# Packing the low half of the softmax weights mid-block, with shifted copies of v, in a fused attention and two-MLP kernel

## The chip, the core and the metric

The kernel runs on one core of one Trainium2 chip. The metric is device time in microseconds (us), the median of several executions; smaller is better. TensorE is written PE (its weight loads PEld), VectorE DVE, ScalarE ACT, GpSimd POOL, SyncE SP. Nearly all DMAs are issued by SP, in order.

## The reference, cut to what matters

For 4 batches of 8 heads with 576 tokens and 64 columns a head:

```
scores = q @ k.T / 8;  cum = cumsum(max(s, 0))
scores = where(causal, -1e9, scores + min(cum[j] - cum[i], 0))
p = exp(scores - max);  p = p / (sum(p) + 1e-9)
x = p @ v                                        # (4, 576, 512)
u = x + real(fft(fft(x, tokens), features))
y = u + relu(layernorm(u) @ w1) @ w2             # first MLP, 512 -> 2048 -> 512
out = y + relu((layernorm(y) * g) @ w3) @ w4     # second MLP
```

The weights w1 to w4 arrive in 64-bit floating point, everything else in float32.

## The kernel before, in words

Accuracy is kept by splitting each float32 operand of a product into a high and a low half in f16 and adding three products: high with high, high with low, low with high.

A pair is two heads of one batch; there are 16. The 576 rows of a pair's attention are five kinds of tile: A0, A1, M, B1 and B0, which see 129, 257, 320, 448 and 576 keys (`EXT`, line 27). A unit is one kind of tile of one head. `emit_qk32` or `emit_qk` makes the scores, `emit_exp` (line 832) lets ACT write the high half of p in f16 and p itself in float32, `emit_lo` (line 856) lets POOL (in batch 1, for B0, DVE) write the low half behind it. The high half fills `NKB` blocks of 128 columns (2, 3, 3, 4, 5), zeros included, and so does the low half. One DMA transpose (line 864, or 872 for both heads of A0, A1 and M) turns all blocks, and `emit_pv` (line 875) multiplies each: three matmuls for each of the `NKB` blocks, 64 columns wide. B0's and B1's p tiles get their zero columns from POOL in each unit (line 843), the others once. The tile `P.v` holds v as 5 blocks of 128 rows, high and low, written by `split_v` (line 1061): ACT the high half, then DVE the low half.

`attn_steps32` runs batches 0 and 1, `attn_steps` batches 2 and 3. `fft_steps` follows each batch, and the first MLP runs on chunks of 256 or fewer rows: `emit_ln` (line 383) normalises a chunk, splits it into `u16` and has it transposed to `unT`; `emit_g1` and `emit_g2` are its two products. While the first MLP of batch b runs, attention and FFT of batch b+1 are interleaved with it. Batch 0's attention has no MLP beside it; in its place DVE, ACT and POOL convert w1 and w2 (class `Weights`, lines 176 to 260). The second MLP (`Weights7`, `emit_g1x`, `emit_g2x`) follows when attention is over; its weights are opened by `open_wb` (line 1377), which closes the attention pools and opens a pool in their place.

The order of instructions on each engine is fixed when the kernel is compiled: a planner simulates the program and sorts by simulated time and priority, and each engine then takes its list in order.

Of the kernel before, what the change touches and what calls it, by code (L numbers as in the profile page):

```python
# [26 lines left out]
EXT = [129, 257, 320, 448, 576]  # L27
NKB = [2, 3, 3, 4, 5]
MASKED = -(2.0 ** 120)
# [4 lines left out]
def fused_kernel(ctx: ExitStack, tc, q, k, v, s, wa1, wa2, g_ln, wb1, wb2, tok_c, feat_c, ident_c, rev_c, bias_c, out):  # L34
    nc = tc.nc

    const = ctx.enter_context(tc.tile_pool(name="const", bufs=1))
    wpool = ctx.enter_context(tc.tile_pool(name="wpool", bufs=1))
# [13 lines left out]
    FW = [130, 258, 320, 448, 576]  # L52
    HW = [512, 768, 768, 1024, 1280]

# [3 lines left out]
    def htile(name, t, h, which):  # L58
        return ring.tile([128, HW[t]], F16, tag=f"h{which}{t}{h}", name=name)

    probs = {}

    def htile2(name, t, which):
        if which:
            return ring.tile([128, 2 * HW[t]], F16, tag=f"h{which}{t}", name=name)
        if t not in probs:
            w = probs[t] = ring.tile([128, 2 * HW[t]], F16, name=f"p16{t}")
            nc.gpsimd.memset(w.rearrange("p (r w) -> p r w", r=4)[:, :, EXT[t]:], 0.0)
        return probs[t]
# [4 lines left out]
    def fwide(name):  # L74
        turn["f"] += 1
        if turn["f"] % 2:
            return ftile(name, B0, turn["f"] // 2 % 2)
        return htile(name, B0, turn["f"] // 2 % 2, 1).bitcast(F32)

# [30 lines left out]
    class Weights:  # L110
# [271 lines left out]

    def emit_ln(ch):
# [18 lines left out]
        nc.vector.tensor_scalar(out=mp, in0=mv[:, :, 0], scalar1=-1.0, scalar2=None, op0=ALU.mult)  # L402
        ch.last = nc.vector.tensor_tensor(out=mb, in0=mp, in1=p, op=ALU.mult)
        yield
        ch.unT = mpool.tile([128, 8, 256], F16, tag="unT", name="unT")
        for j in range(n):
            u16 = mpool.tile([128, 1024], F16, tag="u16", name="u16")
            nc.scalar.activation(
                out=u16[:, 0:512], in_=xs[j], func=AF.Identity, scale=p[:, j:j + 1], bias=mb[:, j:j + 1]
            )  # L410
# [421 lines left out]
    def emit_exp(u, mn):  # L832
# [5 lines left out]
        u.rs = sums[0][:, 2 * (u.k % 2):2 * (u.k % 2) + 2]  # L838
        w = NKB[t] * 128
        if t in (B0, B1):  # L840
# [15 lines left out]
    def emit_lo(u):  # L856
        t = u.t
        n, w = EXT[t], NKB[t] * 128
        eng = nc.gpsimd if t in KN["LO_POOL"][u.p // NPAIR] else nc.vector
# [16 lines left out]
    def emit_pv(u):  # L876
# [7 lines left out]
        ps = pvt[0]  # L884
        nb = NKB[t]
        pT = u.pT[:, 0:2 * nb * 128].rearrange("p (b n) -> p b n", n=128)
        c = slice(64 * h, 64 * h + 64)
        n = 0
        for kb in range(nb):

            for lp, lv in ((0, 0), (0, 1), (1, 0)):
                nc.tensor.matmul(  # L892
                    out=ps[:, c], lhsT=pT[:, lp * nb + kb, :], rhs=P.v[:, kb, lv, c],
                    start=(n == 0), stop=(n == 3 * nb - 1),
                )
                n += 1
        if h == 1:
# [123 lines left out]
    def prep_pair32(p):  # L1021
# [14 lines left out]
        for t in range(4):  # L1036
# [12 lines left out]
        nc.scalar.activation(  # L1049
            out=P.v[:, :, 0, :].bitcast(BF16), in_=rv, func=AF.Square, accum_out=mx[:, 2:3]  # L1050
        )
# [6 lines left out]
    def v_tile():  # L1058
        return att.tile([128, 5, 2, 128], F16, tag="v16", name="v16", bufs=2)

    def split_v(P, rv):
        nc.scalar.activation(out=P.v[:, :, 0, :], in_=rv, func=AF.Copy, scale=P.sc[:, 2:3])
        nc.vector.scalar_tensor_tensor(
            out=P.v[:, :, 1, :], in0=rv, scalar=P.sc[:, 2:3], in1=P.v[:, :, 0, :], op0=ALU.mult, op1=ALU.subtract
        )

    def emit_qk32(u):
# [309 lines left out]
    def open_wb(ch):  # L1377
        att_stack.close()
        wpool2 = ctx.enter_context(tc.tile_pool(name="wpool2", bufs=1))
        gt = const.tile([128, KB], F32, name="gt")  # L1380
        nc.sync.dma_start(out=gt, in_=g_ln.rearrange("(k p) -> p k", p=128))
# [20 lines left out]
    if True:  # L1402
# [59 lines left out]
        first = chunks1(0)  # L1462
        for n, _ in enumerate(urgent(emit_ln(first[0]), KN["LNOFF"][0])):
            weights_after((list(KN["QL"]) + [0] * 9)[n], first[0].last)
        attns = {1: gated(urgent((attn_steps32 if N32 > 1 else attn_steps)(1), KN["A1OFF"]), wa.mark)}
        for b in range(B):
            chunks = first
            if b + 1 < B:
                first = chunks1(b + 1)

                def gens(b=b):
# [97 lines left out]
```

## Time and profile before

| | us |
|---|---|
| median of 3 runs | 1078.03 (1076.03 to 1079.23) |
| the profiled execution, own time | 1075.65 |
| its span, first to last instruction | 1073.9 |
| PE busy | 970.5 (90%), granted clock 0.96 of full |
| DVE, ACT, POOL busy | 670.2, 594.3, 457.5 |

Busy time is that of the engine's own instructions. A wait is idle time of an engine put down to the instruction or DMA that ended it. The clock column is the granted clock of TensorE, 1.00 for 2.4 GHz and 0.50 for 1.2 GHz; a value between is a mean over a stretch that had both.

### The profile page before, as it was taken

How to read it: one execution, taken by the hardware profiler on the slowest of the kernel's cores; microseconds unless marked ns; L12 is line 12 of the kernel's file. 1: busy time of each engine (PE TensorE's matmuls, PEld its weight loads, DVE VectorE, ACT ScalarE, POOL GpSimd, SP SyncE). 2: the span in 40 equal slices, each digit the busy share in tenths (PEclk: the TensorE clock that was granted, in tenths of full speed). 3: DMA queues.
4: the chain of work that ended last, by engine and by line, in shares of the span. 5: the costliest groups of instructions: out<-in, count | busy, mean ns of one | idle time of the engine just before them, and what ended most of it. 6: DMA issues, size and time to landing. Idle time of an engine off the chain costs nothing.

```text
span 1073.9 us, 22892 instructions
## 1 busy us (share of the span) xinstructions
PE 970.5 (90%) x8665; PEld 741.5 (69%) x8665; DVE 670.2 (62%) x1655; ACT 594.3 (55%) x1271; POOL 457.5 (43%) x766
## 2 busy tenths in 40 slices
PE   4677668999989899789999989899999999999998
PEld 3454345777656676457666656578888888888887
DVE  5989878667775564956659978744543553542342
ACT  5788668775686753877534465444444444443341
POOL 3535334555365451535610052454544544543452
PEclk9779877999999999999999999999999999999999
DMA  6999965888589970699934852021112111111000
GB/s 194 268 184 283 219 166 113 175 156 134 118 161 183 205 150 2 138 200 161 207 89 137 294 168 61 21 59 21 41 43 38 40 46 36 40 40 21 21 21 21
DMA packets 289063, 125.47 MB, mean 117 GB/s; under 512 B 272696, under 2 KB 272952, under 8 KB 286904
## 3 DMA queue, kind: packets, MB, share of 16 engines
q1 hardware_dynamic: 288312, 121.90, 51.3%
q0 software_dynamic: 640, 2.10, 0.7%
q8 instruction: 68, 1.11, 0.4%
q14 instruction: 43, 0.35, 0.1%
HBM read 61.50 MB, written 9.51 MB: 66 GB/s over the span
## 4 chain that ended last, share of the span: by engine, by line
PE 38%; DVE 7%; DMA 2%; ACT 2%; issue 1%; SPq 0%; DVEq 0%; ACTq 0%
PE acc L538 15%; PE g1x L510 9%; PE g L510 9%; PE g L468 2%; PE g L444 2%; DMA unT<-u 1%; DVE wblow L189 1%; DMA wbbig<-in_moe_w_ch_dram 1%; DVE wblow L192 1%; DVE h L451 1%; DVE wbbig L369 1%; DVE st L394 0%; ACT wbrows L239 0%; DVE wbrows L192 0%; DMA xset<-x2d 0%
## 5 line engine op out<-in xcount | busy, mean ns | idle before, releaser
L444 PE MATMUL g<-unT,warows 128*128 128x256 f16 (+1 forms) x1920 | 220.9, 266 | 4.3 <-DMA unT<-u 4.3
L444 PEld LDWEIGHTS <-warows 128*128 128x128 f16 x1920 | 175.2, 100 | 44.3 <-DMA unT<-u 3.9
L468 PE MATMUL g<-wastage,h 128*128 128x512 f16 x756 | 184.6, 383 | 10.1 <-ACT h L450 6.7
L510 PEld LDWEIGHTS <-wbrows 128*128 128x128 f16 x1728 | 169.1, 98 | 20.2
L860 POOL TENSOR_TENSOR p<-sc,p 128x448 f16<-128x448 f32 (+4 forms) x152 | 140.5, 934 | 95.5 <-ACT sc L850 79.5
L524 DVE TENSOR_TENSOR wastage<-wastage 128x896 f16<-128x896 f32 x72 | 78.5, 1090 | 161.3 <-ACT wastage L523 161.3
L538 PEld LDWEIGHTS <-wastage 128*128 128x128 f16 x1512 | 147.9, 98 | 17.1
L468 PEld LDWEIGHTS <-h 128*128 128x128 f16 x864 | 83.0, 99 | 101.3 <-DVE h L451 11.8
L523 ACT CAST wastage<-wastage 128x896 f16<-128x896 f32 x72 | 67.5, 938 | 117.1 <-POOL wastage L521 117.1
L849 ACT ACTIVATE p<-sc,mn 128x129 f16<-128x129 f32 (+4 forms) x160 | 89.1, 576 | 46.7 <-DVE mn L816 20.7
L520 POOL TENSOR_TENSOR wastage<-wastage 128x128 f32<-128x128 f32 x72 | 50.5, 702 | 133.9 <-ACT wastage L517 133.9
L510 PE MATMUL g1x<-unT,wbrows 128*128 128x256 f16 x864 | 101.5, 273 | 0.0
L510 PE MATMUL g<-unT,wbrows 128*128 128x256 f16 x864 | 100.9, 273 | 0.0
L892 PEld LDWEIGHTS <-pT 128*128 128x128 f16 x1632 | 64.8, 101 | 47.8 <-DMA pT<-p 30.3
L892 PE MATMUL pv<-v,pT 128*128 128x64 f16 x1632 | 70.6, 198 | 28.0 <-DMA pT<-p 22.7
L850 ACT ACTIVATE sc<-sc,mn 128x129 f32<-128x129 f32 (+4 forms) x160 | 91.6, 573 | 1.1
L538 PE MATMUL acc<-wbbig,wastage 128*128 128x256 f16 x756 | 89.9, 273 | 0.0
L538 PE MATMUL acc<-wblow,wastage 128*128 128x256 f16 x756 | 87.9, 273 | 0.0
L797 POOL TENSOR_SCALAR_AFFINE_SELECT sc<-cumb 128x129 f32<-128x129 f32 (+4 forms) x120 | 63.8, 544 | 46.4 <-ACT cumb L713 30.1
L1084 PE MATMUL s<-first 128*128 128x288 f32 (+4 forms) x192 | 74.7, 489 | 5.0 <-DVE mn L1089 3.5
L451 DVE SCALAR_TENSOR_TENSOR h<-g,h 128x512 f16<-128x512 f32 (+1 forms) x80 | 50.5, 631 | 33.6 <-ACT h L450 33.1
L450 ACT ACTIVATE h<-g 128x512 f16<-128x512 f32 (+1 forms) x80 | 43.4, 543 | 32.3 <-PE g L444 31.9
(238 smaller groups left out, 1529.3 us busy)
## 6 DMA issues: line engine op xcount, KB each, us to landing
wbbig<-in_moe_w_ch_dram SPq DMA_DIRECT2D x8, 1024.0 KB
wbbig<-in_moe_w_ch_dram SPq DMA_DIRECT2D x16, 512.0 KB
cumb<-cumd SPq DMA_DIRECT2D x24, 288.0 KB
wastage<-in_moe_w_ch_dram SPq DMA_DIRECT2D x6, 1024.0 KB
xset<-in_moe_w_ch_dram SPq DMA_DIRECT2D x9, 512.0 KB
x2d<-o SPq DMA_DIRECT2D x18, 256.0 KB
first<-in_q_dram SPq DMA_DIRECT2D x64, 64.0 KB
first<-in_k_dram SPq DMA_DIRECT2D x32, 128.0 KB
```

The source lines that it names most:

```text
L444: nc.tensor.matmul(out=ps[:, c * i:c * i + c], lhsT=ch.w.w1(lw, kk, m + i), rhs=ch.unT[:, 4 * lx + kk, 0:c], start=(n == 0), stop=(n == 23),)
L468: nc.tensor.matmul(out=ch.ps[j], lhsT=h[:, lh, c:c + 128], rhs=ch.w.w2(lw, m + i), start=(m + i + n == 0), stop=(m + i == MB - 1 and n == 2),)
L510: nc.tensor.matmul(out=ps, lhsT=ch.w.w1(lw, kk, m + 8 * half), rhs=ch.unT[:, 4 * lx + kk, :], start=(n == 0), stop=(n == 11),)
L523: nc.scalar.copy(out=h[:, 0], in_=r[:, 0:7])
L524: nc.vector.tensor_tensor(out=h[:, 1], in0=r[:, 0:7], in1=h[:, 0], op=ALU.subtract)
L538: nc.tensor.matmul(out=acc[key], lhsT=h[:, lh, ia], rhs=b[:, ib, lw], start=(m == 0 and i == 0 and not second), stop=(m == 7 and i == 2 an ...
L797: nc.gpsimd.affine_select(out=u.f[:, 0:n], in_=P.cumb[u.h][:, 0:n], pattern=[[-1, n]], compare_op=ALU.is_ge, fill=MASKED, base=base, chann ...
L849: nc.scalar.activation(out=u.w[:, 0:n], in_=u.f[:, 0:n], func=AF.Exp, bias=mn, scale=-1.0)
L850: nc.scalar.activation(out=u.f[:, 0:n], in_=u.f[:, 0:n], func=AF.Exp, bias=mn, scale=-1.0, accum_out=u.rs[:, h:h + 1])
L860: eng.tensor_tensor(out=u.w[:, w:w + n], in0=u.f[:, 0:n], in1=u.w[:, 0:n], op=ALU.subtract)
L892: nc.tensor.matmul(out=ps[:, c], lhsT=pT[:, lp * nb + kb, :], rhs=P.v[:, kb, lv, c], start=(n == 0), stop=(n == 3 * nb - 1),)
L1084: nc.tensor.matmul(out=ps, lhsT=P.qT[:, QCOLS[t]], rhs=P.kT[h][:, a:z], start=not pe, stop=not masked,)
```

## The change

For A0, A1, M and B0 the high half now ends in the middle of a block (`HALF` = 192, 320, 320, 576 columns) and the low half begins there, so that both together take 3, 5, 5 and 9 blocks in place of 4, 6, 6 and 10. B1 stays at 4 and 4. A low half that begins 64 columns into a block meets v shifted by 64 rows, so `P.v` grows from 5 to 9 blocks: DVE copies v's high rows shifted by 64 into blocks 7 and 8, and rows for the one mixed block (`MIX`) into blocks 4 to 6, four copies a pair. A mixed block takes two matmuls (with v's high and its low), a full pair of blocks three as before. B0's p tile now has no zero columns to fill. In `emit_ln`, for the opening chunk of each batch, DVE in place of ACT makes the high half of `u16`, and one small product goes. Tiles are resized, and a few small tiles of the second MLP move to the pool that replaces the attention's.

```diff
-NKB = [2, 3, 3, 4, 5]
+NF = [1, 2, 2, 3, 4]
+HALF = [192, 320, 320, 512, 576]
+MIX = {A0: 5, A1: 6, M: 6, B0: 4}
...
-    HW = [512, 768, 768, 1024, 1280]
+    HW = [384, 640, 640, 1024, 1280]
...
-            nc.gpsimd.memset(w.rearrange("p (r w) -> p r w", r=4)[:, :, EXT[t]:], 0.0)
+            if t != M:
+                nc.gpsimd.memset(w.rearrange("p (r w) -> p r w", r=4)[:, :, EXT[t]:], 0.0)
...
             self.at, self.left = {}, []
+            const = wpool2_[0] if wpool2_ else const_
             self.fro = const.tile([128, 32], F32, name=f"{self.pre}fro")
...
-        ch.last = nc.vector.tensor_tensor(out=mb, in0=mp, in1=p, op=ALU.mult)
+        if not soon:
+            ch.last = nc.vector.tensor_tensor(out=mb, in0=mp, in1=p, op=ALU.mult)
...
+            if soon:
+                nc.vector.tensor_scalar(
+                    out=u16[:, 0:512], in0=xs[j], scalar1=mv[:, j, 0:1], scalar2=p[:, j:j + 1],
+                    op0=ALU.subtract, op1=ALU.mult,
+                )
+            else:
+                nc.scalar.activation(
+                    out=u16[:, 0:512], in_=xs[j], func=AF.Identity, scale=p[:, j:j + 1], bias=mb[:, j:j + 1]
+                )
...
-        w = NKB[t] * 128
+        w = HALF[t]
...
-        for kb in range(nb):
-
-            for lp, lv in ((0, 0), (0, 1), (1, 0)):
-                nc.tensor.matmul(
-                    out=ps[:, c], lhsT=pT[:, lp * nb + kb, :], rhs=P.v[:, kb, lv, c],
-                    start=(n == 0), stop=(n == 3 * nb - 1),
-                )
-                n += 1
+        rows = lambda kb, lv: P.v[:, kb, lv, c]
+        if t == B1:
+            steps = [s for i in range(4) for s in ((i, rows(i, 0)), (i, rows(i, 1)), (4 + i, rows(i, 0)))]
+        else:
+            steps = [s for i in range(f) for s in ((i, rows(i, 0)), (i, rows(i, 1)), (f + 1 + i, rows(7 + i // 2, i % 2)))]
+            steps += [(f, rows(MIX[t], 0)), (f, rows(MIX[t], 1))]
+        for n, (block, vs) in enumerate(steps):
+            nc.tensor.matmul(out=ps[:, c], lhsT=pT[:, block, :], rhs=vs, start=(n == 0), stop=(n == len(steps) - 1))
...
     def split_v(P, rv):
-        nc.scalar.activation(out=P.v[:, :, 0, :], in_=rv, func=AF.Copy, scale=P.sc[:, 2:3])
+        nc.scalar.activation(out=P.v[:, 0:5, 0, :], in_=rv, func=AF.Copy, scale=P.sc[:, 2:3])
+        far = P.v[:, 7:9].rearrange("p i l n -> p (i l) n")
+        nc.vector.tensor_copy(out=far[0:64], in_=P.v[64:128, 0:4, 0])
+        nc.vector.tensor_copy(out=far[64:128], in_=P.v[0:64, 1:5, 0])
         nc.vector.scalar_tensor_tensor(
...
+        nc.vector.tensor_copy(out=P.v[0:64, 5:7], in_=P.v[0:64, 1:3])
+        nc.vector.tensor_copy(out=P.v[64:128, 4:7], in_=P.v[0:64, 0:1].to_broadcast([64, 3, 2, 128]))
...
-        gt = const.tile([128, KB], F32, name="gt")
+        wpool2_.append(wpool2)
+        gt = wpool2.tile([128, KB], F32, name="gt")
...
-        for n, _ in enumerate(urgent(emit_ln(first[0]), KN["LNOFF"][0])):
+        for n, _ in enumerate(urgent(emit_ln(first[0], True), KN["LNOFF"][0])):
...
-                    yield from urgent(emit_ln(first[0]), KN["LNOFF"][b + 1])
+                    yield from urgent(emit_ln(first[0], True), KN["LNOFF"][b + 1])
```

## Rows read from the trace of the kernel before

**Rows 1.** Busy time by stage: stretch, its length, PE, PEld, DVE, ACT, POOL, clock, DMA share.
```profile
20.00:130.00 110.00, 78.22 (x654) 50.33 (x652) 97.13 (x221) 83.68 (x198) 51.48 (x59) 0.83 1.05 241
130.00:166.50 36.50, 20.21 (x130) 13.80 (x128) 29.46 (x106) 21.53 (x53) 11.08 (x25) 0.71 0.66 162
166.50:250.00 83.50, 83.47 (x770) 59.77 (x771) 57.09 (x173) 68.44 (x167) 41.86 (x78) 0.96 0.80 151
250.00:560.00 310.00, 283.28 (x2793) 200.55 (x2790) 197.44 (x609) 191.66 (x451) 142.25 (x242) 0.97 0.76 147
...
720.00:1073.90 353.90, 348.88 (x3196) 312.46 (x3194) 150.93 (x292) 139.42 (x250) 157.94 (x292) 1.00 0.13 35
```

**Rows 2.** PE's waits, 20 to 130 us: us in total, times, longest.
```profile
PE pv L892 <- DMA pT<-p: 14.5, 7, 3.2
PE s L1080 <- DVE mn L1089: 5.4, 5, 2.1
```

**Rows 3.** PE's waits, 166.5 to 560 us.
```profile
PE pv L892 <- DMA pT<-p: 4.7, 4, 2.1
PE g L444 <- DMA unT<-u: 4.3, 3, 2.0
PE g L468 <- ACT h L450: 3.7, 1, 3.7
...
PE pv L892 <- DVE xset L905: 1.8, 1, 1.8
```

**Rows 4.** The p-by-v matmuls in the timeline: start, us, instructions merged (x).
```profile
66.82 1.76 PE L892 MATMUL pv<-v,pT 128*128 128x64 f16 x30 [1.43 <-DVE xset L905]
...
74.39 0.87 PE L892 MATMUL pv<-v,pT 128*128 128x64 f16 x24
```

**Rows 5.** Busy time of line 892 alone on PE, 190 to 550 us.
```profile
190.00:550.00 360.00, 48.22 (x1164) 0.98 0.80 154
```

**Rows 6.** Busy time by engine in one stretch of batch 0's attention; DMA share, GB/s last.
```profile
60.00:80.00 20.00, 18.00 (x165) 12.98 (x166) 16.18 (x50) 16.13 (x37) 6.21 (x11) 0.75 0.92 162
```

**Rows 7.** DVE lines with one source: ns min/median/max of one, first to last start.
```profile
L766 DVE COPY qx<-first x8: 294/398/841, 270.9 to 504.6; 128x512 f16<-128x512 f16 x8
```

**Rows 8.** The same for a tiny DVE instruction.
```profile
L829 DVE TENSOR_SCALAR rs<-rs x40: 147/230/1091, 26.7 to 522.0; 128x4 f32<-128x4 f32 x40
```

**Rows 9.** Timeline around batch 0's opening chunk, ACT, DVE and PE.
```profile
158.27 1.50 ACT L408 ACTIVATE u<-xset,va 128x512 f16<-128x512 f32 x2
...
159.79 0.16 DVE L101 TENSOR_SCALAR wasc<-total 128x1 int32<-128x1 int32 x1 [1.52 <-PE total L92]
...
160.54 0.75 DVE L413 SCALAR_TENSOR_TENSOR u<-un,va,u 128x512 f16<-128x512 f32 x1
...
164.61 1.23 PE L1084 MATMUL s<-first 128*128 128x257 f32 x2 [3.49 <-DVE mn L1089]
166.53 8.27 PE L444 MATMUL g<-unT,warows 128*128 128x256 f16 x48 [0.69 <-DMA unT<-u]
```

**Rows 10.** Timeline around batch 2's opening chunk, ACT and PE.
```profile
437.73 1.50 ACT L408 ACTIVATE u<-xset,va 128x512 f16<-128x512 f32 x2
...
441.50 1.36 PE L468 MATMUL g<-wastage,h 128*128 128x512 f16 x4 [3.66 <-ACT h L450]
...
448.81 2.56 PE L444 MATMUL g<-unT,warows 128*128 128x256 f16 x22 [1.54 <-DMA unT<-u]
```

**Rows 11.** POOL's zero columns of p: busy us, mean ns, idle before, releasers.
```profile
L843 POOL MEMSET p<- 128x128 f16 x64 | 13.0, 205 | 110.3 <-DMA pT<-p 69.4 <-PE ps L1210 31.3 <-DVE rest L639 5.6
```

**Rows 12.** SP's timeline: the load of `gt`, and a transpose of the last batch.
```profile
144.15 0.43 SPq L1381 DMA_DIRECT2D gt<-in_moe_g_ln_dram  x1
...
539.00 1.24 SPq L416 DMA_TRANSPOSE unT<-u  x1
```

**Rows 13.** Readers of the FFT's table `tok`: ns min/median/max, first to last start.
```profile
L1210 PE MATMUL ps<-eo,tok x108: 163/163/191, 134.8 to 556.3; 128*128 128x1 f16 x90, 128*64 128x1 f16 x18
```

**Rows 14.** The first readers of `gt`, same columns.
```profile
L203 ACT ACTIVATE junk<-wbrows,gt x8: 1137/1148/1152, 581.1 to 607.6; 128x1024 bf16<-128x1024 f32 x8
```

More of the change, by code (lines that the diff above doesn't have):

```diff
@@ L35, in fused_kernel @@
     nc = tc.nc
-    const = ctx.enter_context(tc.tile_pool(name="const", bufs=1))
+    const = const_ = ctx.enter_context(tc.tile_pool(name="const", bufs=1))
+    wpool2_ = []
     wpool = ctx.enter_context(tc.tile_pool(name="wpool", bufs=1))
@@ L58, in htile @@
     def htile(name, t, h, which):
-        return ring.tile([128, HW[t]], F16, tag=f"h{which}{t}{h}", name=name)
+        return ring.tile([128, 1152 if t == B0 and which else HW[t]], F16, tag=f"h{which}{t}{h}", name=name)
     probs = {}
@@ L77, in fwide @@
             return ftile(name, B0, turn["f"] // 2 % 2)
-        return htile(name, B0, turn["f"] // 2 % 2, 1).bitcast(F32)
+        return htile(name, B0, turn["f"] // 2 % 2, 1).bitcast(F32)[:, 0:576]
     def hwide(name, t):
@@ L381, in fused_kernel, with emit_ln @@
     un_tile = [lambda: fwide("un")]
-    def emit_ln(ch):
+    def emit_ln(ch, soon=False):
         n = ch.n
@@ L401, in emit_ln @@
         )
-        nc.vector.tensor_scalar(out=mp, in0=mv[:, :, 0], scalar1=-1.0, scalar2=None, op0=ALU.mult)
-        ch.last = nc.vector.tensor_tensor(out=mb, in0=mp, in1=p, op=ALU.mult)
+        ch.last = nc.vector.tensor_scalar(out=mp, in0=mv[:, :, 0], scalar1=-1.0, scalar2=None, op0=ALU.mult)
+        if not soon:
+            ch.last = nc.vector.tensor_tensor(out=mb, in0=mp, in1=p, op=ALU.mult)
         yield
@@ L407, in emit_ln @@
             u16 = mpool.tile([128, 1024], F16, tag="u16", name="u16")
-            nc.scalar.activation(
-                out=u16[:, 0:512], in_=xs[j], func=AF.Identity, scale=p[:, j:j + 1], bias=mb[:, j:j + 1]
-            )
+            if soon:
[7 more added lines that the diff above has]
+                )
             un = un_tile[0]()[:, 0:512]
@@ L857, in emit_lo @@
         t = u.t
-        n, w = EXT[t], NKB[t] * 128
+        n, w = EXT[t], HALF[t]
         eng = nc.gpsimd if t in KN["LO_POOL"][u.p // NPAIR] else nc.vector
@@ L884, in emit_pv @@
         ps = pvt[0]
-        nb = NKB[t]
-        pT = u.pT[:, 0:2 * nb * 128].rearrange("p (b n) -> p b n", n=128)
+        f = NF[t]
+        pT = u.pT[:, 0:2 * HALF[t]].rearrange("p (b n) -> p b n", n=128)
         c = slice(64 * h, 64 * h + 64)
-        n = 0
-        for kb in range(nb):
-            for lp, lv in ((0, 0), (0, 1), (1, 0)):
-                nc.tensor.matmul(
-                    out=ps[:, c], lhsT=pT[:, lp * nb + kb, :], rhs=P.v[:, kb, lv, c],
-                    start=(n == 0), stop=(n == 3 * nb - 1),
-                )
-                n += 1
+        rows = lambda kb, lv: P.v[:, kb, lv, c]
[6 more added lines that the diff above has]
+            nc.tensor.matmul(out=ps[:, c], lhsT=pT[:, block, :], rhs=vs, start=(n == 0), stop=(n == len(steps) - 1))
         if h == 1:
@@ L1049, in prep_pair32 @@
         nc.scalar.activation(
-            out=P.v[:, :, 0, :].bitcast(BF16), in_=rv, func=AF.Square, accum_out=mx[:, 2:3]
+            out=P.v[:, 0:5, 0, :].bitcast(BF16), in_=rv, func=AF.Square, accum_out=mx[:, 2:3]
         )
@@ L1058, in v_tile @@
     def v_tile():
-        return att.tile([128, 5, 2, 128], F16, tag="v16", name="v16", bufs=2)
+        return att.tile([128, 9, 2, 128], F16, tag="v16", name="v16", bufs=2)
     def split_v(P, rv):
-        nc.scalar.activation(out=P.v[:, :, 0, :], in_=rv, func=AF.Copy, scale=P.sc[:, 2:3])
+        nc.scalar.activation(out=P.v[:, 0:5, 0, :], in_=rv, func=AF.Copy, scale=P.sc[:, 2:3])
+        far = P.v[:, 7:9].rearrange("p i l n -> p (i l) n")
+        nc.vector.tensor_copy(out=far[0:64], in_=P.v[64:128, 0:4, 0])
+        nc.vector.tensor_copy(out=far[64:128], in_=P.v[0:64, 1:5, 0])
         nc.vector.scalar_tensor_tensor(
-            out=P.v[:, :, 1, :], in0=rv, scalar=P.sc[:, 2:3], in1=P.v[:, :, 0, :], op0=ALU.mult, op1=ALU.subtract
+            out=P.v[:, 0:5, 1, :], in0=rv, scalar=P.sc[:, 2:3], in1=P.v[:, 0:5, 0, :], op0=ALU.mult, op1=ALU.subtract
         )
+        nc.vector.tensor_copy(out=P.v[0:64, 5:7], in_=P.v[0:64, 1:3])
+        nc.vector.tensor_copy(out=P.v[64:128, 4:7], in_=P.v[0:64, 0:1].to_broadcast([64, 3, 2, 128]))
     def emit_qk32(u):
```

## The prediction

> **What bounds the kernel now.** I read the busy times by stage first, then PE's waits in each stage, then the timeline at the places where those waits lie, and last the durations of instructions like the ones that are added. The stages differ [rows 1]. From 166.5 us on PE is all but full: 83.47 of 83.5 us to 250, 283.28 of 310 to 560, 348.88 of 353.9 at the end. Whatever shortens PE's list there shortens the time. Before 166.5 us it is otherwise. From 20 to 130 us, in batch 0's attention, PE is busy 78.22 of 110 us while DVE has 97.13 and the DMA share is 1.05: DVE and the DMA engines are both nearly full, and PE's largest wait, 14.5 of its 31.8 idle us, is for the transposed p; the next for an engine is 5.4 us for DVE's scores [rows 2]. From 130 to 166.5 us a chain of FFT, layer norm and weight conversion runs, and PE has 20.21 of 36.5 us. After 720 us there is no attention, and the change touches nothing.
>
> **The p-by-v matmuls.** A head's five tiles take 3 x (2+3+3+4+5) = 51 matmuls now and 5+8+8+12+14 = 47 then, so 8 of 102 go for each pair and 128 of 1632 in all. 24 of them ran in 0.87 us, of which the first takes at least 0.19, so one more costs (0.87-0.19)/23 = 29.6 ns; where the clock was lower, 30 took 1.76 us, 58.7 ns each [rows 4]. Twelve pairs lie beside the MLP, where PE is the bound: 96 x 29.6 ns = 2.8 us saved. From the line's own busy time, 48.22/1164 = 41 ns, it would be 4.0 [rows 5]; nothing if attention there waits anyway. I take 2.8, since the 41 holds pipeline ends that overlap other work. The other 32 lie in batch 0, where PE has 31.8 idle us to hide them: I cost them at 0, at most 32 x 58.7 ns = 1.9 us.
>
> **The transposes.** A pair's p has 68 blocks of 128 columns now (a head 4+6+6+8+10) and 60 then. A block is 128 rows of 256 bytes. From 60 to 80 us the DMA engines moved 162 GB/s at a share of 0.92 [rows 6], 3.24 MB or some 12,700 such packets in 0.92 x 20 x 16 = 294 engine-us, an estimate of 23 ns each, taking all of it for packets of that size. Batch 0 saves 4 x 8 x 128 = 4096 packets, 4096 x 23 ns / 16 = 6.0 us of all engines. All of that counts if the DMA engines set the pace from 20 to 130 us, none if DVE does. The wait for pT is 46% of PE's idle time [rows 2], so I take half, 3.0 us. Beside the MLP the pT waits are 4.7 us in all [rows 3]; with 12% fewer blocks I take 0.5 us off, between 0 and 4.7.
>
> **The copies of v.** Each pair gets four f16 copies on DVE, three of 512 elements a partition and one of 768. The nearest row is the copy to qx, 512 elements f16 to f16: 294 ns at best, 398 median, 841 at worst [rows 7]. Four at the median and 0.1 for the longer one are 1.7 us a pair; 1.2 at best, 3.4 at worst. Three pairs of batch 0 have theirs between 20 and 130 us (pair 0's come before), 5.1 us on a DVE that is 88% busy, where it and the DMA engines share the bound. With the pace a little over half DVE's, I take 3.0 us lost; 0 if they fall into its 12.9 idle us, 10.2 if all are at the worst and on the path. This cancels the transposes' gain. Behind a copy on DVE stand the score reductions of the next units, for which ACT's exponentials and PE wait. The two shifted copies also stand ahead of v's low half, which frees the buffer that the next pair's v is loaded into; I cost that at 0, since v is split several units before its first use. Beside the MLP 12 x 1.7 = 20 us go into DVE's idle 139 us (26.4 + 112.6 [rows 1]): 0; if that cover failed it would show in waits like the one for xset, 1.8 us now [rows 3], and I bound the loss by doubling it, 1.8 us.
>
> One more row shows what may make a copy dear: a DVE instruction on 4 elements took 147 ns at best and 1091 at worst, so it was held up, not computing [rows 8]. The Trainium skill, "SBUF — State Buffer", section "SBUF: two separate sides", says that VectorE and GpSimd share one pair of ports as an exclusive lock, which a two-port VectorE instruction must win for its whole duration. Our trace agrees as far as the spread in rows 7 and 8 goes. By that rule each copy may wait for a whole POOL instruction, and POOL for each copy; this is the third rival's mechanism.
>
> **The opening chunks.** For the two halves of a chunk ACT loses two instructions of 0.75 us each (1.50 for two) and DVE gains two; I price DVE's at the 0.75 us of its own 512-column line there [rows 9]. In batch 0 ACT's two high halves ended at 159.77, and DVE sat idle 1.52 us before 159.79, waiting for a weight scale; then it made the low halves. Now its high halves can fill that idle time. But PE's MLP start at 166.53 stands in PE's order behind a score product that itself waited 3.49 us for DVE, and only 0.69 us was waited for unT. I take 0.7 us; the bounds are a gain of 2.2 (idle before 159.79 and that 0.69) and a loss of 1.7, if pair 4's copies, due at the same time, come first. In batch 2 PE waited 3.66 us for an ACT instruction that stood behind the two high halves [rows 10]; without them it comes up to 1.5 us sooner. I take 1.4 of a possible 5.2 (3.66 + 1.54); a loss of 1.5 if DVE's additions delay its half of the same pair. In batches 1 and 3 no such wait is among the large ones: 0.
>
> **POOL, and the tiles that move.** B0's 32 memsets go, 32 x 205 ns = 6.6 us, with about half of their 69.4 us of waits for transposes [rows 11]. POOL is busy 51.48 of 110 and 142.25 of 310 us [rows 1], so this frees what isn't scarce: 0, with up to 1 us gained where a mask stood behind such a wait. The load of gt leaves 144 us [rows 12], since its place now is where the attention's tables lay, and those are read until 556.3 us [rows 13]. It is needed by weight squares from 581.1 us on [rows 14], so I cost it at 0 so long as SP's list has it behind what is urgent; the fourth rival is the other case.
>
> **The sum.** -2.8 (matmuls) -3.0 +3.0 (batch 0: transposes, copies) -0.5 (pT waits) -0.7 -1.4 (openings) = -5.4 us. From the profiled execution's 1075.65 that gives 1070.3; that execution lies 2.4 us below the median of the runs, so against the median I forecast 1078.0 - 5.4 = 1072.6 us, within 1069.5 and 1075.5 by this case alone.
>
> **The rivals.**
>
> First: hidden anyway. The order on every engine is planned anew, attention beside the MLP waits for other things (PE idles 26.7 us from 250 to 560), and the saved 2.8 us turn into idle. For it: those waits are mostly for DMAs and ACT, not for PE's own list [rows 3]. Against it: PE is 91% busy there. Time: 1078.0 - 1 = 1077.
>
> Second: the DMA engines alone set the pace of batch 0. For it: share 1.05 and the 14.5 us [rows 1, 2]. Against it: DVE at 88%. Then 6.0 us are gained in place of 3.0 and the copies cost nothing: 1078.0 - (2.8+6.0+0.5+0.7+1.4) = 1066.6, say 1067.
>
> Third, the other side: the copies are held up. At the worst row, 0.84 us each [rows 7], pairs 1 to 4 put 16 x 0.84 = 13.4 us on DVE before 166.5 us. At DVE's 88% share 11.8 of it would be on the path; less 2.8 for the matmuls and 3.0 for the transposes, 6 us are lost: 1084. It decides from the point where 16 copies x 0.88 cost as much as all gains (2.8+3.0+0.5+0.7+1.4 = 8.4 us), 0.60 us a copy. For it: the spread of rows 7 and 8. Against it: the median of 398 ns.
>
> Fourth: gt's load is placed early in SP's list and holds it until 556.3 us. The transpose at 539.00 [rows 12] and what follows would come 17 us later; PE has FFT and MLP work of its own for about half of it, so some 9 us are lost less 5.4: about 1082. The planner simulates such waits, which speaks against it.
>
> **How the numbers follow.** Forecast 0.45, hidden 0.23, DMA pace 0.12, held-up copies 0.13, gt 0.07. A change under 0.3% (3.2 us) can't be told from none. Faster by more, below 1074.8: four fifths of the forecast's 0.45, the DMA pace's 0.12 and a little of the hidden case, 0.53. Slower, above 1081.3: 0.20, nearly all of the third and fourth. Same: 0.27. The range reaches from the DMA case to just short of the held-up copies, 1066 to 1083.
>
> **What would show it.** Right: 1504 matmuls on the p-by-v line, 30 ns each; 64 copies on DVE with a median near 0.4 us; unchanged time from the start of the MLP's weight conversion on; a first MLP matmul between 164 and 168 us; at batch 2's opening a wait shorter by 1.4. Wrong: copies at 0.6 us or more with the first MLP matmul after 170 us (third rival), that matmul before 162 us (second), or a gap of PE between 540 and 560 us with SP held by gt (fourth). A difference that comes mostly from after 560 us would be none of these.

## The result, and the profile after

The changed kernel takes 1086.08 us in the median (1083.65 to 1089.01), the kernel before beside it 1077.72: ratio 1.0084, 95% interval 1.0058 to 1.011. It is slower by some 8 to 9 us, where a gain of 5.4 was forecast. Its profiled execution has a span of 1082.3 us, 8.4 above that of before.

Three places in the trace divide the span, and I use them for every run below: the first MLP matmul (its row in the timeline, as in [rows 9]), the end of the last FFT product of batch 3 (matmul `z<-feat`), and the first matmul of the second MLP's second product (`acc<-wbbig`). From there on every kernel here needs the same 351 us.

| us | first MLP matmul | from it to the last `z` | from `z` to first `acc` | span |
|---|---|---|---|---|
| before | 166.5 | 394.6 | 161.8 | 1073.9 |
| after | 169.7 | 397.4 | 164.2 | 1082.3 |

So 3.2 us are lost in batch 0, 2.8 while the first MLP and the attention of batches 1 to 3 run together, and 2.4 in the conversion of the second MLP's weights. Each row is one execution, and two executions of the same lists differ too: the run that moves only small tiles (below) has PE's list of the kernel before to the last matmul, and gave 165.9, 397.1 and 162.0. A difference of 2 or 3 us in one stage can therefore not be read alone; the medians carry the argument.

The busy times of the same stretches as [rows 1] (length, PE, PEld, DVE, ACT, POOL, clock, DMA share, GB/s), in the changed kernel:

```profile
20.00:130.00 110.00, 72.10 (x587) 46.05 (x586) 97.37 (x226) 83.50 (x197) 54.47 (x60) 0.83 1.00 237
130.00:166.50 36.50, 23.84 (x149) 15.41 (x149) 31.43 (x92) 17.93 (x47) 7.23 (x15) 0.65 0.50 120
166.50:250.00 83.50, 81.92 (x715) 58.07 (x715) 62.38 (x208) 69.32 (x166) 40.11 (x70) 0.97 0.80 141
250.00:560.00 310.00, 279.94 (x2714) 196.40 (x2715) 214.84 (x640) 188.18 (x445) 138.78 (x223) 0.97 0.72 141
```

From 250 to 560 us DVE is busy 17.4 us more than in [rows 1], and PE 3.3 us less. PE's 3.3 are about the size of the matmuls that went, and the idle time they left was not used. From 20 to 130 us DVE is as busy as before and PE 6.1 us less.

The p-by-v matmuls and the four copies by their lines (ns min/median/max of one, first to last start), and the matmuls' busy time from 190 to 550 us, which answers [rows 5]:

```profile
L907 PE MATMUL pv<-v,pT x1504: 189/193/261, 30.5 to 542.7; 128*128 128x64 f16 x188
L1075 DVE COPY v<-v x16: 289/290/589, 16.7 to 513.2; 64x512 f16<-64x512 f16 x16
L1076 DVE COPY v<-v x16: 286/288/613, 17.0 to 513.5; 64x512 f16<-64x512 f16 x16
L1080 DVE COPY v<-v x16: 275/282/766, 18.6 to 516.8; 64x512 f16<-64x512 f16 x16
L1081 DVE COPY v<-v x16: 546/546/547, 18.9 to 517.5; 64x768 f16<-64x768 f16 x16
```

```profile
190.00:550.00 360.00, 43.57 (x1074) 40.46 (x1074) 0.98 0.77 146
```

The change does what it says: 1504 matmuls and 64 copies. At the medians a pair's copies take 290 + 288 + 282 + 546 ns = 1.41 us, less than the 1.7 forecast from [rows 7]. None of the copies' prices is the surprise.

What changed is who waits. ACT's waits from 20 to 560 us for a row's minimum `mn` (the score reduction on DVE), ahead of the exponential that writes p: the kernel before, then after (us in total, times, longest):

```profile
ACT p L849 <- DVE mn L816: 20.7, 12, 3.0
ACT p L849 <- DVE mn L1089: 15.8, 16, 2.5
```

```profile
ACT p L861 <- DVE mn L1105: 28.2, 17, 3.1
ACT p L861 <- DVE mn L828: 26.7, 15, 4.7
```

36.5 us became 54.9. One such place in batch 0, five successive rows of DVE and then one of ACT, from the timeline of the changed kernel (start, us, instruction, idle before and releaser):

```profile
89.41 0.29 DVE L1075 COPY v<-v 64x512 f16<-64x512 f16 x1
89.72 0.29 DVE L1076 COPY v<-v 64x512 f16<-64x512 f16 x1
90.04 0.89 DVE L1077 SCALAR_TENSOR_TENSOR v<-first,scs,v 128x640 f16<-128x640 f32 x1
90.84 2.06 DVE L194 SCALAR_TENSOR_TENSOR wastage<-wastage 128x1024 int32<-128x1024 int32 x1
92.82 0.48 DVE L1105 CUSTOM_DVE_ANT_0 sc<-s,zero 128x320 f32<-128x320 f32 x1
```

```profile
93.34 0.56 ACT L861 ACTIVATE p<-sc,mn 128x320 f16<-128x320 f32 x1 [3.07 <-DVE mn L1105]
```

The copies stand in DVE's list ahead of the next reduction at 92.82, and ACT idles 3.07 us for it. The two copies push it back by the 0.6 us that they take; the split of v (0.89) and a step of the weight conversion (2.06) stand there too. PE's largest waits from 20 to 130 us, answering [rows 2]:

```profile
PE pv L907 <- DMA pT<-p: 11.5, 5, 6.7
PE s L1096 <- DVE mn L1105: 6.9, 8, 1.7
PE pv L907 <- DVE xset L916: 5.6, 5, 1.9
```

The wait for the transposes fell by the 3.0 us that was forecast (14.5 to 11.5). The waits for DVE took their place: 1.5 us more for `mn`, and 5.6 for `xset`, which had 1.9 before. Beside the MLP the same, from 166.5 to 560 us, answering [rows 3]:

```profile
PE pv L907 <- DMA pT<-p: 7.2, 6, 2.3
PE s L826 <- DVE mn L828: 6.5, 9, 2.1
```

The wait for `mn` was 1.1 us there before, and the wait for pT grew instead of shrinking: p comes later.

### The profile page after: what moved, and what is told of

It is laid out like the page before. It is cut to its first block, busy times and chain, and to the rows that moved or that the text cites. A ratio compares the mean times of both kernels' runs of the same rounds, so it can differ in the third digit from the quotient of the medians.

```text
span 1082.3 us, 22634 instructions
## 1 busy us (share of the span) xinstructions
PE 971.0 (90%) x8537; PEld 738.1 (68%) x8537; DVE 698.9 (65%) x1723; ACT 589.4 (54%) x1263; POOL 450.8 (42%) x733
## 4 chain that ended last, share of the span: by engine, by line
PE 46%; DVE 15%; DMA 5%; issue 4%; ACT 4%; POOL 2%; SPq 1%; POOLq 0%; DVEq 0%; ACTq 0%
PE acc L550 15%; PE g L522 9%; PE g1x L522 9%; PE g L456 6%; PE g L480 5%; DMA first<-first 1%; POOL p L872 1%; DVE h L463 1%; DVE wblow L197 1%; DMA pT<-p 1%; PE pv L907 1%; PE y L1208 1%; DVE sc L828 1%; DMA unT<-u 1%; PE z L1245 1%
## 5 line engine op out<-in xcount | busy, mean ns | idle before, releaser
L536 DVE TENSOR_TENSOR wastage<-wastage 128x896 f16<-128x896 f32 x72 | 78.4, 1089 | 161.5 <-ACT wastage L535 161.5
L480 PEld LDWEIGHTS <-h 128*128 128x128 f16 x864 | 83.4, 99 | 94.5 <-DVE h L463 12.6
L861 ACT ACTIVATE p<-sc,mn 128x576 f16<-128x576 f32 (+4 forms) x160 | 89.5, 576 | 64.8 <-DVE mn L1105 28.2
L907 PEld LDWEIGHTS <-pT 128*128 128x128 f16 x1504 | 59.5, 101 | 50.1 <-DMA pT<-p 29.0
L862 ACT ACTIVATE sc<-sc,mn 128x576 f32<-128x576 f32 (+4 forms) x160 | 91.7, 574 | 1.2
L907 PE MATMUL pv<-v,pT 128*128 128x64 f16 x1504 | 64.1, 197 | 30.9 <-DMA pT<-p 20.4
L1100 PE MATMUL s<-first 128*128 128x288 f32 (+4 forms) x192 | 72.4, 476 | 4.5 <-DVE first L1044 2.4
```

What stands on the lines that cost most here:

```text
L480: nc.tensor.matmul(out=ch.ps[j], lhsT=h[:, lh, c:c + 128], rhs=ch.w.w2(lw, m + i), start=(m + i + n == 0), stop=(m + i == MB - 1 and n == 2),)
L536: nc.vector.tensor_tensor(out=h[:, 1], in0=r[:, 0:7], in1=h[:, 0], op=ALU.subtract)
L861: nc.scalar.activation(out=u.w[:, 0:n], in_=u.f[:, 0:n], func=AF.Exp, bias=mn, scale=-1.0)
L862: nc.scalar.activation(out=u.f[:, 0:n], in_=u.f[:, 0:n], func=AF.Exp, bias=mn, scale=-1.0, accum_out=u.rs[:, h:h + 1])
L907: nc.tensor.matmul(out=ps[:, c], lhsT=pT[:, block, :], rhs=vs, start=(n == 0), stop=(n == len(steps) - 1))
L1100: nc.tensor.matmul(out=ps, lhsT=P.qT[:, QCOLS[t]], rhs=P.kT[h][:, a:z], start=not pe, stop=not masked,)
```

## The experiments

The theories: **A**, the copies lengthen attention's chain (in a finer form **A1**, by DVE's time alone, against **A2**, by the waits of those who read them); **B**, the opening chunks' high half on DVE; **C**, the new order of the lists, which the planner sorts anew after any edit; **D**, the small tiles that moved. Each median stands with its ratio to the kernel before on the same chip and its 95% interval. The code shown is cut; "..." marks what is left out.

**Opening chunks put back.** In the changed kernel:

```diff
-        for n, _ in enumerate(urgent(emit_ln(first[0], True), KN["LNOFF"][0])):
+        for n, _ in enumerate(urgent(emit_ln(first[0]), KN["LNOFF"][0])):
...
```

> The changed kernel with ACT making the opening chunks' high halves again, as before; everything about p and v is kept. Theory A (the copies of v, 25.4 us of DVE work, lengthen the chain of attention, which is late by 5 to 10 us from 297 us on): 1084 to 1088. Theory B (the opening chunks' high half on DVE is what delays the attention beside it): 1072 to 1078. Theory C (the planner sorts every engine's list anew, and the sort costs or gives some us whatever the edit is): anywhere from 1072 to 1090, with the lateness at another place than in the changed kernel.

1086.51 us, 1.0096 (1.0073 to 1.0119). **Opening chunks alone**, the edit of `emit_ln` in the kernel before:

```diff
-        for n, _ in enumerate(urgent(emit_ln(first[0]), KN["LNOFF"][0])):
+        for n, _ in enumerate(urgent(emit_ln(first[0], True), KN["LNOFF"][0])):
...
```

> The kernel before with only the opening chunks' edit in emit_ln. Theory A (copies): 1076 to 1079, no change. Theory B (opening chunks): 1082 to 1088. Theory C (the new sort): anywhere from 1072 to 1090, though DVE gains only 8 instructions of about 0.55 us and ACT loses 8.

1076.20 us, 0.9991 (0.9973 to 1.0008). B falls: against their neighbours, 1086.08 and 1076.75, the two differ by 0.4 and 0.6 us, less than can be measured. In both, about a quarter of PE's list up to the last `z` stands in another order, and the time did not move; that sizes C as small here, which later runs correct.

**No copies.** The four copies go; a low block then meets the unshifted v, which leaves the shifted rows out of the product:

```diff
-            steps = [s for i in range(f) for s in ((i, rows(i, 0)), (i, rows(i, 1)), (f + 1 + i, rows(7 + i // 2, i % 2)))]
-            steps += [(f, rows(MIX[t], 0)), (f, rows(MIX[t], 1))]
+            steps = [s for i in range(f) for s in ((i, rows(i, 0)), (i, rows(i, 1)), (f + 1 + i, rows(i, 0)))]
+            steps += [(f, rows(f, 0)), (f, rows(f, 1))]
...
-        nc.vector.tensor_copy(out=far[0:64], in_=P.v[64:128, 0:4, 0])
...
```

> The changed kernel without the four copies of v; the matmuls read blocks of v that are there, so the shifted rows are left out of the product; all instruction counts but the 64 copies are the changed kernel's. Theory A (copies): 1070 to 1077, the whole 8.4 us or more come back. Theory B (opening chunks): 1083 to 1087. Theory C (the new sort): anywhere from 1070 to 1090.

1066.89 us, 0.9909 (0.9885 to 0.9934): 19.2 us below the changed kernel (18.8 by the two ratios) and 9.9 below before. More came back than A's 1070 to 1077. A stands, so far for one order of the lists: nearly half of PE's rows up to the last `z` stand elsewhere than in the changed kernel. Its three stages are 161.5, 386.4 and 163.0 us: the copies cost 8.2 us in batch 0, 11.0 beside the MLP, 1.2 after. ACT's waits for `mn` without the copies:

```profile
ACT p L861 <- DVE mn L828: 17.9, 11, 3.1
ACT p L861 <- DVE mn L1100: 13.7, 11, 2.2
```

31.6 us, below the 36.5 of before. **Small tiles alone**, moved in the kernel before; PE's, DVE's and ACT's order stays:

```diff
-        gt = const.tile([128, KB], F32, name="gt")
+        gt = wpool2.tile([128, KB], F32, name="gt")
```

> The kernel before with only the small tiles of the second MLP (gt and those of columns) moved into the pool that opens when attention closes; the order on PE, DVE and ACT stays that of before, and one DMA and one memset move. Theory D (the later load of gt and the later memset cost the 2 to 3 us that were lost between 580 and 690 us): 1079.5 to 1081.5, with the loss between 560 and 690 us. Theories A to C: 1077 to 1079, no change.

1076.43 us, 1.0 (0.9984 to 1.0016). D falls.

**Copies that nobody reads.** All four on DVE, the matmuls as in the run without copies; the order of the lists is that of the changed kernel, but for two rows of PE and some 36 of DVE's 1449 up to the last `z`. The last copy goes where nothing is read:

```diff
-        nc.vector.tensor_copy(out=P.v[64:128, 4:7], in_=P.v[0:64, 0:1].to_broadcast([64, 3, 2, 128]))
+        nc.vector.tensor_copy(out=P.v[64:128, 6:9], in_=P.v[0:64, 0:1].to_broadcast([64, 3, 2, 128]))
```

> All four copies stay on DVE in their places, but the p-by-v matmuls read only the five blocks that were there before (the shifted rows are left out of the product, as in the kernel without copies), so nobody waits for a copy. Theory A1 (the copies cost DVE time on the chain of scores, row maxima and exponentials; 25.4 us of them and some 5 us of DVE's waits for v's high half ahead of the first): 1083 to 1088, like the changed kernel. Theory A2 (the matmuls, or the tile v for the next pair, wait for the copies, and DVE's time itself is covered): 1066 to 1072.

1086.44 us, 1.0084 (1.0065 to 1.0103), the changed kernel's time. A2 falls: with the lists as they are here, nobody's wait for a copy costs anything. **Each copy twice**:

```diff
         nc.vector.tensor_copy(out=far[0:64], in_=P.v[64:128, 0:4, 0])
         nc.vector.tensor_copy(out=far[64:128], in_=P.v[0:64, 1:5, 0])
+        nc.vector.tensor_copy(out=far[0:64], in_=P.v[64:128, 0:4, 0])
...
```

> The changed kernel with each of the four copies issued twice in a row: 64 more DVE instructions, some 25 us more. Theory A1: another 15 to 25 us, 1100 to 1110. Theory A2: about 1.4 us later for a pair's first matmul, mostly covered by the units between, 1086 to 1092. If only a new sort of the lists had cost the time: anywhere, 1070 to 1095.

1104.92 us, 1.0249 (1.0224 to 1.0274). With 0, 64 and 128 copies the kernel takes 1066.9, 1086.4 (nobody reads) or 1086.1 (read), and 1104.9: 19.5 and 18.5 us for the two steps of 64. The three kernels have three orders, about half of PE's rows up to the last `z` apart; that both steps come out alike speaks for the copies, though the order alone can move some us (below). The copies of the changed kernel take 25.4 us in sum, so three quarters of each us on DVE reach the end, as a mean over the kernel. ACT's waits for `mn` don't grow in step, to 57.9 us only, and over the runs that follow they don't sort the times: 49.1 us in the one with batch 0's copies alone (1076.89), 38.2 in the one whose later pairs are read (1079.51). That the time is lost by way of these waits is therefore argued, not shown; which link of the chain takes it is open.

**Copies by DMA**, from SP, and **by POOL**, all four of them:

```diff
-        nc.vector.tensor_copy(out=far[0:64], in_=P.v[64:128, 0:4, 0])
+        nc.sync.dma_start(out=far[0:64], in_=P.v[64:128, 0:4, 0])
...
```

```diff
-        nc.vector.tensor_copy(out=far[0:64], in_=P.v[64:128, 0:4, 0])
+        nc.gpsimd.tensor_copy(out=far[0:64], in_=P.v[64:128, 0:4, 0])
...
```

> The changed kernel with the four copies as DMAs from SP (per pair some 512 pieces of 256 bytes and 256 of 512 to 1024; the transposes saved 1024 pieces). Theory A1: DVE is free of them, 1064 to 1074, in batch 0 about 4 to 6 us dearer than without any copy, as the DMA share there is near 1. Theory A2: the DMAs land later than DVE's copies would, 1084 to 1092.

> The changed kernel with the four copies on POOL. POOL is 42% busy, but makes the low halves of p. Theory A1: 1067 to 1078, depending on POOL's own price a copy (0.4 to 1.2 us). Theory A2: 1084 to 1092, since POOL's copies are later.

1079.74 us, 1.0036 (1.002 to 1.0051), and 1082.24 us, 1.0056 (1.0036 to 1.0076). Both are cheaper than on DVE, and both miss A1's numbers: the other queues are not free either. Stages: 165.7, 399.0, 161.6 with DMAs, 161.3, 407.0, 160.1 with POOL. On POOL they cost batch 0 nothing and the stage beside the MLP 21 us against the run without copies. The instructions on `v` with the copies on POOL (first three rows), and what waited (last row):

```profile
L1075 POOL COPY v<-v x16: 604/636/1257, 16.4 to 513.3; 64x512 f16<-64x512 f16 x16
L1077 DVE SCALAR_TENSOR_TENSOR v<-first,scs,v x16: 844/1098/1297, 16.6 to 514.0; 128x640 f16<-128x640 f32 x16
L1076 POOL COPY v<-v x16: 608/746/1444, 17.1 to 513.9; 64x512 f16<-64x512 f16 x16
...
  POOL v L1075: 27.4, 7
```

POOL stood idle 27.4 us in seven places ahead of the first copy, waiting for ACT's high half of v, with its low halves of p behind it in its list. On DVE that wait was 5.1 us in seven places. The DMAs took SP some 0.6 us each to issue (median 639 ns for the first), in the list that also issues the transposes; that this is their cost was not tested.

**Where the cost lies.** Copies that nobody reads, made by the twelve pairs of batches 1 to 3 alone, and by batch 0's four alone:

```diff
+        later = all(P is not pairs[i] for i in range(NPAIR))
+        if later:
...
```

```diff
+        later = any(P is pairs[i] for i in range(NPAIR))
+        if later:
...
```

> As the kernel in which nobody waits for a copy, but batch 0's four pairs make no copies; the twelve pairs of batches 1 to 3, which lie beside the MLP, keep theirs (48 copies, 17 us). The forecast's costing (beside the MLP DVE has idle time enough, 0): 1066 to 1068, the time without copies. Theory A1 (the copies lie on attention's own chain there too): 1066.9 + 11 to 14 = 1078 to 1081, by the lateness that the changed kernel gathered after its first MLP matmul or by 12/16 of the whole.

> The counterpart of the run without batch 0's copies: nobody waits for a copy, and only batch 0's four pairs make them (16 copies, 5.6 us of DVE). Forecast's costing: +3.0, 1070. If every one of these copies lies on the path there (DVE 90% busy from 20 to 130 us): 1066.9 + 6 to 8 = 1073 to 1075, and the rest of the 13.1 us between the run with all idle copies and the run with the later twelve pairs' comes only where both are present. If the two parts simply add up: 1080.

1073.34 us, 0.9974 (0.9956 to 0.9993): 6.4 above the run without copies. 1076.89 us, 1.0004 (0.9985 to 1.0022): 10.0 above. Both times lie between the alternatives that were expected, in none of them. Stages 164.2, 393.3, 163.1 and 169.5, 387.9, 163.4. So batch 0's sixteen copies cost 8.0 us up to the first MLP matmul, more than their own 5.6, and 1.5 beside the MLP; the later 48 cost 6.9 beside it, and 2.7 before it, where pair 4's four lie. The 1.5 and the 2.7 are no more than single executions differ by. Read by the matmuls, **the later twelve pairs'** cost more:

```diff
+        far = u.p >= NPAIR
+        mix = MIX[t] if far and t != B1 else f
...
```

> As the run with the copies of the later twelve pairs alone (1073.3), but there the matmuls read the copies as in the changed kernel (batch 0's still read the unshifted blocks, which leaves its shifted rows out). The work on every engine is the same, its order on the lists differs in about a third of PE's rows. If only DVE's time counts: 1072 to 1075, and the 1087.1 of the whole kernel with POOL's copies in batch 0 is POOL's doing. If a new sort or the waits of the later pairs' matmuls cost: 1080 to 1087.

1079.51 us, 1.0038 (1.0016 to 1.0059), just below the range expected if a new order or readers' waits cost; stages 162.6, 398.9, 163.2. With the same work and a third of PE's rows up to the last `z` in another order it is 6.2 us above the other run of these pairs. Since readers' waits cost nothing at equal order, this is most likely C's size: some 6 us.

One difference of two kernels is thus worth little, but there are three for each part. The later 48 copies cost 6.4 us (added to no copies, unread), 12.6 (added to no copies, read) and 9.6 (added to batch 0's: 1086.44 less 1076.89). Batch 0's sixteen cost 10.0 (added to no copies), 13.1 (added to the later ones, unread: 1086.44 less 1073.34) and 6.6 (added to them, read: 1086.08 less 1079.51). All six are losses of 6 us or more. The split is therefore 7 to 13 us for batch 0 and 6 to 13 for the rest, no finer.

**128 matmuls more**, a third one for each mixed block in the run without copies:

```diff
-            steps += [(f, rows(f, 0)), (f, rows(f, 1))]
+            steps += [(f, rows(f, 0)), (f, rows(f, 1)), (f, rows(f, 1))]
```

> The kernel without copies with the 128 p-by-v matmuls put back (each mixed block gets a third matmul, which adds a low product a second time). The forecast's costing (PE's list is the bound beside the MLP): 1066.9 + 2.8 = 1069.7. Theory A1 (attention's chain is the bound there and PE has slack): 1066 to 1068.

1066.20 us, 0.991 (0.9882 to 0.9938), as without them. This is no test of what 128 matmuls cost: over a quarter of PE's rows up to the last `z` stand in another order, which can move more than the 2.8 us in question, and the stages, 158.0, 388.9 and 161.7, are 3.5 us shorter before the MLP and 2.5 longer beside it.

**Fewer copies.** Two a pair, with the mixed block's high tail in two matmuls of 64 rows (`lo` is rows 0 to 63), then the same with batch 0's on POOL:

```diff
-            steps += [(f, rows(MIX[t], 0)), (f, rows(MIX[t], 1))]
...
+            steps += [(f, P.v[lo, f, 0, c], lo), (f, P.v[lo, f, 1, c], lo), (f, P.far[:, 0, c])]
...
+            k = part[0] if part else slice(0, 128)
+            nc.tensor.matmul(out=ps[:, c], lhsT=pT[k, block, :], rhs=vs, start=(n == 0), stop=(n == len(steps) - 1))
...
```

> The changed kernel with two copies a pair in place of four (one of 512 and one of 640 elements a partition, about 0.65 us in place of 1.40): the mixed block takes its high tail against the unshifted v in two matmuls of 64 rows and the low head against one shifted block with zeros above it, 51 matmuls a head as before the change. Theory A1, linear in DVE's time: 1066.9 + 19.2 x 0.65/1.40 = 1075.8, up to 2.8 more if the matmuls count. If the number of copies counted, and not their time: 1076.5.

> The same with batch 0's two copies a pair on POOL. With all copies on POOL the first MLP matmul came as early as without any copy, 8.4 us before the changed kernel's, so batch 0's share goes: 1075.8 less 3.7 = 1072, at best 1070, at worst 1076 if POOL's copies hold up its low halves. This would beat both kernels.

1099.67 us, 1.0228 (1.0196 to 1.0259), and 1091.38, 1.0148 (1.0117 to 1.0179). Both missed, for a reason outside the theories: the p-by-v matmuls of the first one, by form (busy us, mean ns), then of the run without copies:

```profile
L910 PE MATMUL pv<-v,pT 128*128 128x64 f16 x1376 | 83.1, 199 | 24.2 <-DMA pT<-p 14.4 <-DVE scs L110 2.7 <-ACT v L1084 2.5
L910 PE MATMUL pv<-v,pT 64*128 64x64 f16 x256 | 31.0, 200 | 0.0
```

```profile
L907 PE MATMUL pv<-v,pT 128*128 128x64 f16 x1504 | 64.7, 197 | 20.8 <-DMA pT<-p 13.4 <-DVE xset L916 6.7 <-ACT first L1030 0.5
```

114.1 us of PE in place of 64.7, for 128 matmuls more. Neither kernel computes the reference's product, for a cause that was not found; their times price these instructions as they were issued, and say nothing of the copies. With all matmuls at 128 rows, and the mixed blocks' copies **cut to v's high half**:

```diff
-        nc.vector.tensor_copy(out=P.v[0:64, 5:7], in_=P.v[0:64, 1:3])
+        nc.vector.tensor_copy(out=P.v[0:64, 5:7, 0], in_=P.v[0:64, 1:3, 0])
...
-            steps += [(f, rows(MIX[t], 0)), (f, rows(MIX[t], 1))]
+            steps += [(f, rows(MIX[t], 0)), (f, rows(f, 1))]
```

> The changed kernel with the mixed blocks' copies cut to v's high half (256 and 384 elements a partition in place of 512 and 768), the low half of the mixed block read where it lies unshifted: about 1.0 us a pair in place of 1.40, all matmuls 128 rows. Linear in DVE's time: 1066.9 + 19.2 x 1.0/1.40 = 1080.6. If the number of copies counted: 1086.

1079.25 us, 1.0022 (1.0005 to 1.0039), near the 1080.6 expected if the cost goes with the copies' time, where their number gave 1086. But the trace does not bear that reading out. The two smaller copies:

```profile
L1080 DVE COPY v<-v x16: 209/211/1055, 18.3 to 512.5; 64x256 f16<-64x256 f16 x16
L1081 DVE COPY v<-v x16: 284/286/1014, 19.1 to 514.8; 64x384 f16<-64x384 f16 x16
```

Their medians fell as hoped, but 17 of the 64 copies took 398 to 1055 ns, and in sum the copies took 24.8 us after 25.4. So the 6.8 us gained are not the price of DVE's time saved; a quarter of PE's rows up to the last `z` stand in another order, and that alone can move as much.

**Batch 0's copies on POOL**, in the changed kernel, then with the smaller copies:

```diff
+        eng = nc.gpsimd if any(P is pairs[i] for i in range(NPAIR)) else nc.vector
-        nc.vector.tensor_copy(out=far[0:64], in_=P.v[64:128, 0:4, 0])
+        eng.tensor_copy(out=far[0:64], in_=P.v[64:128, 0:4, 0])
...
```

> The changed kernel, whole, with batch 0's copies on POOL and the others on DVE. The run with the later twelve pairs' copies alone took 1073.3, and with all copies on POOL the first MLP matmul came as early as without copies: 1072 to 1076. If POOL's copies hold up its low halves of p: 1078 to 1082.

> Both: the smaller copies, batch 0's on POOL. 1073.3 less 6.4 x 0.4/1.4 = 1071.5, between 1069 and 1075: under both kernels. If POOL's copies hold up its low halves of p: 1077 to 1080.

1087.07 us, 1.0093 (1.0073 to 1.0114), and 1077.84, 1.0006 (0.9991 to 1.0022). The second missed its 1069 to 1075 and came out where it was expected if POOL's copies hold up its low halves of p. The first missed by 11 us: its first MLP matmul came at 164.3, 5.4 earlier than in the changed kernel, and its next stage took 405.8, 8.4 more. **The first again, with ACT making the opening halves**, an edit that moved the time by 0.4 and 0.6 us above:

```diff
-        for n, _ in enumerate(urgent(emit_ln(first[0], True), KN["LNOFF"][0])):
+        for n, _ in enumerate(urgent(emit_ln(first[0]), KN["LNOFF"][0])):
...
```

> The whole changed kernel with batch 0's copies on POOL, and ACT making the opening chunks' high halves as before the change (an edit that was worth 0.4 us or less in two comparisons, but sorts the lists anew). If POOL's copies in batch 0 cost what the gain at the first MLP matmul gave: 1085 to 1089. If the 1087.1 was the sort of that kernel: 1073 to 1082.

1077.96 us, 1.0025 (1.0003 to 1.0048); stages 163.0, 399.7, 163.2. So 9 us of the 1087.07 (7 by the two ratios) most likely belong to that kernel's order. No kernel with the whole new packing beats the one before; the nearest, 1077.84, can't be told from it.

## Why the prediction was wrong

**The step that failed** is "Beside the MLP 12 x 1.7 = 20 us go into DVE's idle 139 us (26.4 + 112.6 [rows 1]): 0". It rests on "PE is all but full", taken from PE's share, 91% from 250 to 560 us. The runs showed a loss of 6 to 13 us for these pairs in place of 0 (bound 1.8), in each of three comparisons. So DVE's time there is not covered: 48 copies, 20 to 23 us in sum, put 0.3 to 0.55 of their time on the end. Whether PE's time counts there too was not shown. By the waits the loss goes through attention's own chain: scores, minima on DVE, exponentials on ACT, transposes, product; PE would then fill the chain's gaps with the MLP, and look full for it. No run isolates this chain. The sign was in [rows 1, 3]: a bound engine has no 26.7 us of waits for others.

**The second term** too small is batch 0's: +3.0 us for the copies, measured 8.2 (changed kernel) or 8.0 (those copies alone) at the first MLP matmul, and 7 to 13 by the times. I had given DVE "a little over half" of the pace there; with it 88% busy, all of the copies' 5.6 us and more counted. In sum the copies were costed at 3.0 and cost 19.2. **A third** thing stood in no sum: the prediction names the new order of the lists, in its first rival, but gives it no price. Two pairs of kernels of the same work, or nearly the same, differed by 6.2 and 9.1 us, so the range of 3 us to either side was too narrow for any such change.

**The rest of the sum** came out, in part by luck. Without the copies it says -2.8 - 3.0 - 0.5 - 0.7 - 1.4 = -8.4 us, and the run without copies gave -9.9 (-12.4 to -7.1 by its interval). But with the 128 matmuls put back, where the sum says -5.6, it was -10.1, so the 2.8 for the matmuls is not borne out, and one order of the lists can hide it. By place it was less exact: the stages before the first MLP matmul gained 5.0 (forecast 3.7), the one beside the MLP 8.2 (4.7). Whether the shorter transposes, POOL's missing memsets or the order gave the surplus was not tested. At batch 2's opening PE's wait of 3.66 us [rows 10] is gone in the changed kernel; the one for `unT` stayed:

```profile
440.76 1.03 PE L480 MATMUL g<-wastage,h 128*128 128x512 f16 x4
...
447.98 7.03 PE L456 MATMUL g<-unT,warows 128*128 128x256 f16 x48 [1.41 <-DMA unT<-u]
```

It moved nothing that the two runs on the openings could measure.

**The rivals.** The third came nearest with 1084, by another way: it wanted copies of 0.60 us or more, held up by POOL, and they took 0.40 on average (25.4 / 64), each line's median within 7 ns of its minimum. Ten copies were held up by POOL, all after 200 us, for 2.9 us in sum (last section): the mechanism is real and too small. Its reckoning that DVE's time reaches the end nearly whole was right for batch 0, where it stopped. The first (hidden anyway) has the run with the 128 matmuls put back for it, but that run can't decide 2.8 us. The second fell: batch 0's transposes wait shrank by 3.0, not 6, and the copies there were not free. The fourth fell with the run that moves `gt` alone. The first MLP matmul came at 169.7, outside the 164 to 168 named, and that sign alone pointed at the copies. The 2.4 us lost after the last `z` are of the size by which that stage varies over all runs here, 160.1 to 164.5 us, with no work of it changed; it is left open what sorts them.

## What to carry to other kernels

An engine that is 91% busy, much of it with filler work, need not be the only bound: ask whose end the stage waits for, and don't cost what is added to another engine of that chain at nothing because the engine looks idle (here 0.3 to 0.55 of its time counted beside the MLP, all of it and more in batch 0, three quarters in the mean). Before trading DMA pieces and matmuls for instructions on VectorE, take the added instructions out in one run and double them in another; two runs gave here the cost by linearity. Read the instructions' sum, not their medians. Where a planner sorts every list anew, two kernels with the same work differed by 6 to 9 us, so a step smaller than that wants two orders of it.

## What the runs showed of the hardware

A few matmuls of 64 rows between matmuls of 128 rows are dear: 128 groups of two put PE's p-by-v time from 64.7 to 114.1 us, and the 128-row matmuls around them rose from 43 ns each (64.7 / 1504) to 60 (83.1 / 1376). The Trainium skill, "TensorEngine Tiling (Array Packing)", section "Tiling Modes", says that a change of tiling mode drains TensorE. The trace agrees in that such groups cost time, (114.1 - 64.7 - 128 x 0.03) / 128 = 0.36 us each as an estimate, with 0.03 us for a plain matmul from [rows 4]; that a drain takes it no trace here shows.

With POOL's copies beside it, DVE's split of v (line 1077) took 1098 ns in the median; in the changed kernel, where POOL has none, it took 885:

```profile
L1077 DVE SCALAR_TENSOR_TENSOR v<-first,scs,v x16: 884/885/1321, 17.3 to 513.9; 128x640 f16<-128x640 f32 x16
```

The Trainium skill, "SBUF — State Buffer", section "SBUF: two separate sides", has VectorE instructions with two inputs in SBUF and GpSimd's reads exclude one another for a whole instruction; these two medians agree with it. The plain copies wait too. POOL and then DVE in the changed kernel:

```profile
207.19 0.56 POOL L809 TENSOR_SCALAR_AFFINE_SELECT sc<-cumb 128x448 f32<-128x448 f32 x1
```

```profile
207.30 0.59 DVE L1075 COPY v<-v 64x512 f16<-64x512 f16 x1 [1.44 <-ACT v L1073]
```

Ten of the 48 copies of 512 elements took 389 to 766 ns in place of 275 to 299. Each began while a POOL instruction ran, and ended 141 to 151 ns after that instruction did, so it waited out POOL. (One that began at 93.96 us was not held, beside a POOL row that ran on; POOL's rows are rough.) The sixteen of 768 elements took 546 or 547 ns each, with POOL running or not. When these were cut to 384 elements, in the run with the smaller copies, some of them waited as well (286 ns in the median, 1014 at most): a smaller copy is not a shorter one for certain.
